# Operand sums of a seven-product scheme on GpSimd, sums of squares in PSUM, and more chunks in that scheme

## The chip, the cores and the metric

The kernel runs on one core of a Trainium2 chip. The metric is the device time of one execution in microseconds (us); a run's time is compared by the median of several executions. A core has five engines with a queue each, which run at the same time and wait for one another by semaphores: TensorE (PE in the profile, with its weight loads as PEld), VectorE (DVE), ScalarE (ACT), GpSimd (POOL) and SyncE (SP). In this kernel SP issues the stores and the DMA transposes, GpSimd issues the loads. SBUF is the working memory of 128 partitions; PSUM holds the matmuls' results in 8 banks of 128 x 2 KB.

## The reference

Four batches of 5824 rows with 256 columns go through a channel attention, and its result through a small network without nonlinearity:

```python
qn = q / (np.linalg.norm(q, axis=1, keepdims=True) + 1e-06)
kn = k / (np.linalg.norm(k, axis=1, keepdims=True) + 1e-06)
s = kn.transpose(0, 2, 1) @ qn / tau          # 256 x 256 per batch
a = softmax(s)
x = (v @ a).reshape(B * S, D)
h = (x @ w1) * (x @ w2) @ w3                  # w1, w2: 256 x 1024, w3: 1024 x 1024
out = h @ w_out                               # 1024 x 256
```

## The kernel before

The product of w3 and w_out is computed once (`w_unit`, the result is `W_sb`, 1024 x 256). For each batch the softmax matrix is multiplied into w1 and w2 (`fold`, the results are `Wf`), so that a row of the output takes two steps: a and b, each 256 to 1024 columns, their elementwise product `abh`, and `abh` times `W_sb`, called o.

**Chunks and slots.** The time is laid out by hand: the order in which the Python code emits instructions is the order in every queue. Batch b (0 to 3) has twelve chunks c: eleven of 512 rows and a small one of 192 (128 rows, and 64 rows that are paired over two batches). A chunk has eight slots, one for each 128 of the 1024 columns. In a slot `emit_ab` issues four matmuls of 512 columns into two of the four PSUM banks `ab0` to `ab3` (L587), a ScalarE copy of a to bf16 (`as`, L593) and VectorE's product with b (`abh`, L604, 128x512). Bank use comes round after two slots: a of slot s+2 overwrites a of slot s.

**The second step of a chunk** is put into a list `pend` and taken out in later slots. In a usual chunk `emit_out` adds four matmuls of 256 columns per slot (L634), 32 in all, into two PSUM tiles of the tag `out` (three banks), which ScalarE and VectorE then copy out (L655, L656), and SP stores.

**Seven products.** In the chunks that `seven(b, c)` names (four each in b=1 and b=2, ten in b=3) the second step is done by a Strassen-like scheme with seven products of half size in place of eight: `seven_products`. Each product is eight matmuls of 128 columns (L518), so 56 matmuls of 128 columns. It needs four sums of `abh` tiles (128x1024 bf16, `sum1`, and at the head of p1, p5 and p7; L534 to L551, on VectorE), combined weights (`combine_weights`, once, at the start of b=1), four ScalarE copies of a product to the output tile (`keep`, L528) and three VectorE adds (`join`, L531). Products called A, B and C take the three `out` banks. The sums share two tiles `S12` and `S34` in the pool of large tiles.

**Scores of the next batch.** While batch b runs, the 23 pairs of row blocks of batch b+1 go into the 256 x 256 score matrix: a pair is cut into units, `pair_unit`: parts 0 and 1 each have two G matmuls of 256 columns (L201) and a ScalarE square of 128x512 (L198), and in part 2 VectorE adds the squares of 128x1024 f32 to `acc` in SBUF (L210). In b=0 they are laid out by a modelled clock from 54 to 113; in b=1 and 2 by slots 4 to 71 with a weight per slot from `scores_of`, which gives few or none near a chunk of seven products. Then `norms` adds the two halves of `acc` on VectorE, GpSimd sums over the partitions (`tot`, L271, a library routine), and a chain of small steps on ScalarE and VectorE (`k_row` to `exps`) and the folds follow, at fixed distances of the modelled clock (`k_row` 5.5 after `norms`).

**GpSimd's queue** holds the loads of q, k and v. Ahead of a load stands a `gate`, a copy of one element of the latest `abh`, so that the load isn't issued before that slot, and after a load of v a `hold`, a copy of one element of the transposed v, before the next load. Transposes and stores stand in SP's queue in the order of the code.

The pool of large tiles has 22 buffers of 4 KB per partition; pieces of q, k, v and the `abh` halves come from it.

Of the kernel before, what the change touches and what calls it, by code (L numbers as in the profile page):

```python
# [12 lines left out]
F32 = DT.float32  # L13
# [6 lines left out]
BIG_BUFS = 22  # L20
# [5 lines left out]
def kernel(  # L26
# [46 lines left out]
    turns = [0]  # L73

    def bank(tag):

        if tag == "out":
            return {"tag": "out", "bufs": 3}
        turns[0] += 1
        return {"tag": f"ab{turns[0] % 4}", "bufs": 1}  # L80
# [99 lines left out]
    def score_units(n):  # L180
# [4 lines left out]
        def pair_unit(pr, part):  # L185
# [3 lines left out]
            if pr == 0 and part == 0:  # L189
                G_tiles[n] = psum.tile([P, CT, C], F32, tag="G", name=f"G_{n}", bufs=1)  # L190
                accs[n] = work.tile([P, 2, 2, C], F32, tag="acc", name=f"acc_{n}", bufs=1)
            G = G_tiles[n]
            if part < 2:
                if part == 0 and pr > 0:
                    sqs[0] = work.tile([P, 2, 2, C], F32, tag="sq", name=f"sq_{n}_{pr}", bufs=2)
                dst = accs[n] if pr == 0 else sqs[0]
                src = qt if part == 0 else kt
                nc.scalar.activation(out=dst[:, :, part, :], in_=src[:, o : o + 2, :], func=AF.Square)  # L198
# [10 lines left out]
            elif pr > 0:  # L209
                nc.vector.tensor_add(accs[n], accs[n], sqs[0])  # L210

        sqs = [None]
        for pr in range(npair):
            for part in range(3):
# [11 lines left out]
    def squares(nm, pi, slots, end=False):  # L226

        if nm not in S:
            S[nm] = psum.tile([P, CT, P], F32, tag="out", name=f"sq{nm}_0", bufs=3)
# [22 lines left out]
    def soft_units(n):  # L252
# [14 lines left out]
        def norms():  # L267
            a1 = work.tile([P, 2, C], F32, tag="acc1", name=f"acc1_{n}", bufs=1)
            nc.vector.tensor_add(a1, accs[n][:, 0], accs[n][:, 1])
# [65 lines left out]
        def sum_start():  # L335
            st["sum"] = psum.tile([P, 512], F32, tag="out" if n == 0 else "G", name=f"sum_{n}", bufs=3 if n == 0 else 1)
# [128 lines left out]
    slot = [0]  # L465
    comb = {}

    def seven(b, c):
        return c < NCH - 2 if b == B - 1 else b > 0 and c in (0, 1, 4, 7)

    def scores_of(b, s):

        j = s % FT
        after = s >= FT and seven(b, s // FT - 1)
        if (after and j < 4) or (seven(b, s // FT) and j >= FT - 2):
            return 0.0
        return 0.4 if after and j < FT - 1 else 1.0

    def combine_weights(step):
# [3 lines left out]
        if step == 0:  # L483
            comb["T"] = in_pool.tile([P, 4, 4, P], BF16, tag="big", name="comb_T", bufs=BIG_BUFS)
            for nm in ("S12", "S34"):
                comb[nm] = in_pool.tile([P, 2, 4, 2 * P], BF16, tag="big", name=f"comb_{nm}", bufs=BIG_BUFS)
# [13 lines left out]
    def seven_products(b, c, k1, k2):  # L500
# [4 lines left out]
        s1, s2 = comb["S12"][:, 0], comb["S12"][:, 1]  # L505
        s3, s4 = comb["S34"][:, 0], comb["S34"][:, 1]
# [4 lines left out]
        st = {}  # L511

        def product(nm, a, w, first=False):
            if first:
                st[nm] = psum.tile([P, 2, P], F32, tag="out", name=f"prod{nm}_{b}_{c}", bufs=3)
# [17 lines left out]
        def sum1():  # L533
# [381 lines left out]
```

## Time and profile before

| | |
|---|---|
| median of 3 runs | 563.87 us (563.73 to 564.94) |
| the profiled execution | 564.48 us |
| its span, first to last instruction | 562.7 us |
| granted TensorE clock | 1.000 |
| instructions of PE / DVE / ACT / POOL | 4180 / 693 / 683 / 163 |
| loads from memory, stores | 78.9 MB, 23.9 MB |

Up to about 46 us the first batch's q and k are loaded and their scores computed; from there to the end the slots run. b=0 ends near 181 us, b=1 near 310, b=2 near 441. In the page's list of groups a line gives line, engine, operation, output<-inputs, shapes, count, busy us and mean ns of one instruction, and after the second bar the engine's idle time ahead of it and what ended it. A matmul's mean ns is its latency: matmuls overlap, and the distance from one to the next is shorter.

### The profile page before, as it was taken

What the parts mean: (1) busy time and instruction counts of PE and PEld (TensorE: products, weight loads), DVE (VectorE), ACT (ScalarE), POOL (GpSimd) and SP (SyncE); (2) the same over time, 40 slices, a digit from 0 to 9 for tenths busy, and PEclk for the clock granted to TensorE, in tenths of its full rate; (3) what the DMA queues carried; (4) which work ended last, traced back from release to release, by engine and by line L of the source; (5) the groups of instructions that cost most, each with busy time, mean ns of one, the idle gap of its engine ahead of it and who ended that gap; (6) DMA issues with size and microseconds to landing.
All of it is one profiled execution on the core that took longest, in us unless ns stands there. A gap on an engine that the chain in (4) does not pass through costs nothing.

```text
span 562.7 us, 11089 instructions
## 1 busy us (share of the span) xinstructions
PE 552.9 (98%) x4180; PEld 356.8 (63%) x4187; DVE 424.9 (76%) x693; ACT 355.8 (63%) x683; POOL 79.8 (14%) x163
## 2 busy tenths in 40 slices
PE   8899999999999999999999999999999999999997
PEld 5764566776656566666666666666665666666665
DVE  1046745888876989899876699899877688888884
ACT  1046535777765778788665667778656566665663
POOL 4260013111021111120030100202030000100000
PEclk9999999999999999999999999999999999999999
DMA  9999899978555676675664576675760153340102
GB/s 213 212 181 209 151 179 232 224 170 187 146 127 137 122 157 137 133 162 116 150 155 109 123 161 149 138 172 86 176 133 37 76 122 76 109 94 38 76 38 93
DMA packets 75108, 77.51 MB, mean 138 GB/s; under 512 B 54192, under 2 KB 58800, under 8 KB 75056
## 3 DMA queue, kind: packets, MB, share of 16 engines
q0 software_dynamic: 15760, 38.93, 40.1%
q1 hardware_dynamic: 59008, 37.23, 21.9%
q10 hardware_dynamic: 288, 0.66, 0.4%
q8 instruction: 32, 0.52, 0.3%
q14 instruction: 20, 0.16, 0.1%
HBM read 78.91 MB, written 23.86 MB: 183 GB/s over the span
## 4 chain that ended last, share of the span: by engine, by line
PE 90%; DMA 7%; POOL 1%; DVE 1%; ACT 1%; issue 0%; POOLq 0%
PE b L587 27%; PE a L587 27%; PE o L634 17%; PE prodA L518 6%; PE G L201 5%; DMA k<-in_k_dram 5%; PE prodC L518 3%; DMA v<-in_v_dram 2%; PE fold L370 2%; PE prodB L518 1%; PE w L760 1%; POOL w L729 0%; DVE abh L604 0%; ACT as L593 0%; POOL w L728 0%
## 5 line engine op out<-in xcount | busy, mean ns | idle before, releaser
L604 DVE TENSOR_TENSOR abh<-as,b 128x512 bf16<-128x512 bf16 x352 | 240.8, 685 | 88.8 <-ACT as L593 82.5
L593 ACT CAST as<-a 128x512 bf16<-128x512 f32 (+1 forms) x384 | 216.3, 563 | 126.2 <-PE a L587 96.3
L587 PEld LDWEIGHTS <-Wf 128*128 128x128 bf16 x1536 | 144.4, 98 | 104.1 <-issue 1.7
L587 PE MATMUL a<-vT,Wf 128*128 128x512 bf16 x704 | 209.4, 379 | 0.5 <-ACT Wf L403 0.4
L587 PE MATMUL b<-vT,Wf 128*128 128x512 bf16 x704 | 209.4, 379 | 0.2 <-DVE abh L604 0.2
L634 PE MATMUL o<-W_sb,abh 128*128 128x256 bf16 x832 | 123.0, 273 | 0.0
L634 PEld LDWEIGHTS <-abh 128*128 128x128 bf16 x832 | 81.0, 98 | 41.7 <-issue 0.2
L210 DVE TENSOR_TENSOR acc<-acc,sq 128x1024 f32<-128x1024 f32 x66 | 80.4, 1219 | 0.6 <-ACT sq L198 0.6
L518 PEld LDWEIGHTS <-comb_S 128*128 128x128 bf16 x576 | 38.2, 98 | 17.0 <-DVE comb_S L534 0.2
L201 PE MATMUL G<-k,q 128*128 128x256 bf16 x276 | 48.3, 273 | 0.0
L198 ACT ACTIVATE sq<-q 128x512 f32<-128x512 bf16 x66 | 41.9, 634 | 0.0
L198 ACT ACTIVATE sq<-k 128x512 f32<-128x512 bf16 x66 | 41.5, 628 | 0.0
L528 ACT COPY osb<-prodA 128x256 f32<-128x256 f32 x72 | 26.8, 373 | 21.3 <-PE prodA L518 21.3
L518 PEld LDWEIGHTS <-abh 128*128 128x128 bf16 x432 | 28.7, 98 | 12.7
L575 POOL COPY gate_t<-abh 1x1 bf16<-1x1 bf16 x39 | 11.5, 295 | 157.1 <-DVE abh L604 156.3
L579 POOL COPY gate_t<-vT 1x1 bf16<-1x1 bf16 x16 | 4.4, 277 | 174.0 <-DMA vT<-v 174.0
L201 PEld LDWEIGHTS <-q 128*128 128x128 bf16 x276 | 26.4, 98 | 4.1
L518 PE MATMUL prodA<-comb_T,comb_S 128*128 128x128 bf16 x288 | 22.0, 219 | 0.0
L257 DVE TENSOR_TENSOR dk<-sqk,ident 128x256 f32<-128x256 f32 x1 | 0.4, 424 | 23.9 <-PE sqk L234 23.9
L656 DVE COPY osb<-o 128x512 f32<-128x512 f32 x26 | 17.8, 686 | 0.9 <-PE o L634 0.9
L598 DVE TENSOR_TENSOR left<-as,b 128x192 bf16<-128x192 bf16 x32 | 11.3, 353 | 9.5 <-ACT as L593 7.6
L655 ACT COPY osb<-o 128x512 f32<-128x512 f32 x26 | 15.2, 586 | 3.2 <-PE o L634 2.1
(116 smaller groups left out, 400.1 us busy)
## 6 DMA issues: line engine op xcount, KB each, us to landing
out_dram<-osb SPq DMA_DIRECT2D x44, 512.0 KB, 3.0
k<-in_k_dram POOLq DMA_DIRECT2D x19, 512.0 KB, 8.1
v<-in_v_dram POOLq DMA_DIRECT2D x19, 512.0 KB, 6.0
q<-in_q_dram POOLq DMA_DIRECT2D x18, 512.0 KB, 5.5
w_wout<-in_moe_w_dram POOLq DMA_DIRECT2D x1, 2048.0 KB, 23.8
k<-in_k_dram POOLq DMA_DIRECT2D x4, 320.0 KB, 7.6
v<-in_v_dram POOLq DMA_DIRECT2D x4, 320.0 KB, 4.7
q<-in_q_dram POOLq DMA_DIRECT2D x3, 320.0 KB, 4.5
```

Source lines behind the costliest of these rows:

```text
L198: nc.scalar.activation(out=dst[:, :, part, :], in_=src[:, o : o + 2, :], func=AF.Square)
L201: nc.tensor.matmul(G[:, ct, :], lhsT=qt[:, i, ct * P : (ct + 1) * P], rhs=kt[:, i, :], start=(pr == 0 and part == 0 and ct == 0), stop=(pr ...
L210: nc.vector.tensor_add(accs[n], accs[n], sqs[0])
L518: nc.tensor.matmul(st[nm][:, i, :], lhsT=a[:, j, i * P : (i + 1) * P], rhs=w[j], start=(first and j == 0 and i == 0), stop=(j == 3), skip_ ...
L528: nc.scalar.copy(quarter(r, d), st["A"])
L575: nc.gpsimd.tensor_copy(gate_t, last_ab[0][:1, :1])
L587: nc.tensor.matmul(t[:, :n], lhsT=Wf[b][:, ct, w, j * P : (j + 1) * P], rhs=rhs_of(b, c, ct), start=(ct == 0), stop=(ct == CT - 1),)
L593: nc.scalar.copy(a_sb[:, :n], tiles[0][:, :n])
L604: nc.vector.tensor_mul(ab, a_sb, tiles[1])
L634: nc.tensor.matmul(tl[h][:, o, :], lhsT=lhsT, rhs=W_sb[:, j, :], start=(j == 0 and o == 0), stop=(j == FT - 1 and (small or o == 1)), skip ...
L655: nc.scalar.copy(o[:, 0:2, :], tl[0])
L656: nc.vector.tensor_copy(o[:, 2:4, :], tl[1])
```

## The change

- The four sums of a chunk have a tile each in the pool `work` (`S1` to `S4`, one buffer). In b=0 to 2 GpSimd computes them, from a list `due_sums`, one every two slots from the chunk's end; in b=3 VectorE does, as before.
- The chunks in the scheme: 7 and 8 in b=0, 0 to 7 in b=1 and b=2, ten in b=3 as before.
- In b=0 to 2 the products begin four slots later (`LAG_FAST`), in the order p1, p6, p5, p7, p4, p3, p2, one per slot; joins run at the start of the next slot (`following`). A takes the bank `out0`, B and C `out1`.
- The sums of squares are kept in PSUM, in the third bank (`out2`), and added by VectorE in two halves of 128x512 (parts 2 and 3 of a pair). `norms` copies them with ScalarE.
- Usual chunks of b=0 to 2 (not the small one) go by `emit_half`: the first two row blocks over four slots into `out0`, then the other two into `out1`.
- Scores lie evenly over slots 42 to 78 in b=0 and 4 to 71 in b=1 and 2. The combined weights move from b=1 to b=0, the second step in b=0 starts after slot 31, some loads are moved by a few us, and the large pool has 21 buffers.

```diff
@@ -17,7 +17,8 @@
 PIECE = 8
 LAG = 2
 LAG_END = 5
-BIG_BUFS = 22
+LAG_FAST = 4
+BIG_BUFS = 21
...
-        if tag == "out":
-            return {"tag": "out", "bufs": 3}
-        turns[0] += 1
-        return {"tag": f"ab{turns[0] % 4}", "bufs": 1}
+        turns[tag] += 1
+        return {"tag": f"{tag}{turns[tag] % (4 if tag == 'ab' else 3)}", "bufs": 1}
...
-                accs[n] = work.tile([P, 2, 2, C], F32, tag="acc", name=f"acc_{n}", bufs=1)
+                accs[n] = psum.tile([P, 2, C], F32, tag="out2", name=f"acc_{n}", bufs=1)
...
             if part < 2:
-                if part == 0 and pr > 0:
+                if part == 0:
                     sqs[0] = work.tile([P, 2, 2, C], F32, tag="sq", name=f"sq_{n}_{pr}", bufs=2)
-                dst = accs[n] if pr == 0 else sqs[0]
                 src = qt if part == 0 else kt
-                nc.scalar.activation(out=dst[:, :, part, :], in_=src[:, o : o + 2, :], func=AF.Square)
+                nc.scalar.activation(out=sqs[0][:, :, part, :], in_=src[:, o : o + 2, :], func=AF.Square)
                 i = o + part
...
-            elif pr > 0:
-                nc.vector.tensor_add(accs[n], accs[n], sqs[0])
+            elif pr == 0:
+                if part == 2:
+                    nc.vector.tensor_add(accs[n], sqs[0][:, 0], sqs[0][:, 1])
+            else:
+                nc.vector.tensor_add(accs[n], accs[n], sqs[0][:, part - 2])
 
         sqs = [None]
         for pr in range(npair):
-            for part in range(3):
+            for part in range(4):
                 units.append((0.22 if part < 2 else 0.0, lambda pr=pr, part=part: pair_unit(pr, part)))
         return units
...
         def norms():
             a1 = work.tile([P, 2, C], F32, tag="acc1", name=f"acc1_{n}", bufs=1)
-            nc.vector.tensor_add(a1, accs[n][:, 0], accs[n][:, 1])
+            nc.scalar.copy(a1, accs[n])
...
     def seven(b, c):
-        return c < NCH - 2 if b == B - 1 else b > 0 and c in (0, 1, 4, 7)
-
-    def scores_of(b, s):
-
-        j = s % FT
-        after = s >= FT and seven(b, s // FT - 1)
-        if (after and j < 4) or (seven(b, s // FT) and j >= FT - 2):
-            return 0.0
-        return 0.4 if after and j < FT - 1 else 1.0
+        return c < NCH - 2 if b == B - 1 else c in (FAST if b > 0 else FAST0)
...
         if step == 0:
             comb["T"] = in_pool.tile([P, 4, 4, P], BF16, tag="big", name="comb_T", bufs=BIG_BUFS)
-            for nm in ("S12", "S34"):
-                comb[nm] = in_pool.tile([P, 2, 4, 2 * P], BF16, tag="big", name=f"comb_{nm}", bufs=BIG_BUFS)
             comb["f"] = in_pool.tile([P, 2, 4, P], F32, tag="big", name="comb_f", bufs=BIG_BUFS)
...
@@ -502,17 +497,17 @@
         T = comb["T"]
...
-        s1, s2 = comb["S12"][:, 0], comb["S12"][:, 1]
-        s3, s4 = comb["S34"][:, 0], comb["S34"][:, 1]
...
-        st = {}
+        st, sums = {}, {}
+        tags = {"A": "out0", "B": "out1", "C": "out1" if b < B - 1 else "out2"}
+        adder = nc.vector if b == B - 1 else nc.gpsimd
 
         def product(nm, a, w, first=False):
             if first:
-                st[nm] = psum.tile([P, 2, P], F32, tag="out", name=f"prod{nm}_{b}_{c}", bufs=3)
+                st[nm] = psum.tile([P, 2, P], F32, tag=tags[nm], name=f"prod{nm}_{b}_{c}", bufs=1)
             for j in range(4):
                 for i in range(2):
                     nc.tensor.matmul(
@@ -530,44 +525,62 @@
         def join(nm, r, d):
             nc.vector.tensor_add(quarter(r, d), st[nm], quarter(r, d))
 
-        def sum1():
-            nc.vector.tensor_add(s1, a21, a22)
+        def operand(i):
+
+            x = sums[i] = work.tile([P, 4, 2 * P], BF16, tag=f"S{i}", name=f"S{i}_{b}_{c}", bufs=1)
+            if i == 1:
+                adder.tensor_add(x, a21, a22)
+            else:
+                u, w = {2: (sums.get(1), a11), 3: (a11, a21), 4: (a12, sums.get(2))}[i]
+                adder.tensor_sub(x, u, w)
...
         def p5():
-            nc.vector.tensor_sub(s3, a11, a21)
-            product("C", s1, t1, True)
+            product("C", sums[1], t1, True)
 
         def p6():
-            product("A", s2, t2)
+            product("A", sums[2], t2)
             keep(0, 1)
 
         def p7():
-            nc.vector.tensor_sub(s4, a12, s2)
-            product("A", s3, t3)
+            product("A", sums[3], t3)
             keep(1, 1)
 
         def p2():
-            join("C", 1, 1)
             product("B", a12, w21, True)
 
         def p4():
-            join("B", 0, 0)
             product("A", a22, t4)
             keep(1, 0)
 
         def p3():
-            product("C", s4, w22)
-            join("C", 0, 1)
+            product("C", sums[4], w22)
+
+        def store():
             rows = out[b * N : b * N + NT * P, :].rearrange("(p i) c -> p i c", i=NT)
             nc.sync.dma_start(out=rows[:, 4 * c : 4 * c + 4, :], in_=st["o"])
 
-        return [sum1, p1, p5, p6, p7, p2, p4, p3]
+        def S(i):
+            return lambda: operand(i)
+
+        def J(*x):
+            return lambda: join(*x)
+
+        def then(fn):
+            return lambda: following.append(fn)
+
+        if b == B - 1:
+            return [S(1)], [
+                [S(2), p1], [S(3), p5], [p6], [S(4), p7], [J("C", 1, 1), p2],
+                [J("B", 0, 0), p4], [p3, J("C", 0, 1), store],
+            ]
+        return [S(1), S(2), S(3), S(4)], [
+            [p1], [p6], [p5], [p7, then(J("C", 1, 1))], [p4], [p3, then(J("C", 0, 1))], [p2, then(J("B", 0, 0)), then(store)],
+        ]
...
         if not seven(b, c):
-            pend.append((slot[0] + (FT if 0 < b < B - 1 else LAG), 1, lambda only=None: emit_out(b, c, j, ab, only)))
+            if b == B - 1 or c == NCH - 1:
+                lag = LAG if b == B - 1 else FT + LAG_FAST
+                pend.append((slot[0] + lag, 1, lambda only=None: emit_out(b, c, j, ab, only)))
+            elif j == FT - 1:
+                for i in range(FT):
+                    fn = lambda i=i, ab2=tuple(halves): emit_half(b, c, i, ab2)
+                    pend.append((slot[0] + 1 + LAG_FAST + i, 1, fn))
         elif j == FT - 1:
-            fns = seven_products(b, c, *halves)
-            fns[0]()
-            pend.extend((slot[0] + 1, 2, fn) for fn in fns[1:])
+            sums, groups = seven_products(b, c, *halves)
+            for i, fn in enumerate(sums):
+                due_sums.append((slot[0] + 2 * i, fn))
+            ready = slot[0] + 1 + (LAG_FAST if b < B - 1 else 0)
+            for i, group in enumerate(groups):
+                wait = 0 if b == B - 1 else i + (i == 6)
+                pend.append((ready + wait, 2, lambda group=group: [fn() for fn in group]))
         clock[0] += 4 * (n * MM_COL + MM_FIX)
+
+    def emit_half(b, c, i, ab2):
+
+        h, jj = divmod(i, 4)
+        if i % 4 == 0:
+            out_tiles[b, c, h] = psum.tile([P, 2, D], F32, tag=f"out{h}", name=f"o_{b}_{c}_{h}", bufs=1)
+        if i == 0:
+            out_tiles[b, c] = work.tile([P, 4, D], F32, tag="o_sb", name=f"osb_{b}_{c}", bufs=3)
+        t, o = out_tiles[b, c, h], out_tiles[b, c]
+        for j in (2 * jj, 2 * jj + 1):
+            for k in range(2):
+                nc.tensor.matmul(
+                    t[:, k, :], lhsT=ab2[j // 4][:, j % 4, (2 * h + k) * P : (2 * h + k + 1) * P], rhs=W_sb[:, j, :],
+                    start=(j == 0 and k == 0), stop=(j == FT - 1), skip_group_check=True,
+                )
+        clock[0] += 4 * (D * MM_COL + MM_FIX)
+        if i == 3:
+            nc.scalar.copy(o[:, 0:2, :], t)
+        elif i == FT - 1:
+            nc.vector.tensor_copy(o[:, 2:4, :], t)
+            rows = out[b * N : b * N + NT * P, :].rearrange("(p i) c -> p i c", i=NT)
+            nc.sync.dma_start(out=rows[:, 4 * c : 4 * c + 4, :], in_=o)
 
...
         if j == 0:
             out_tiles[b, c] = [
-                psum.tile([P, 2, D], F32, tag="out", name=f"o_{b}_{c}_{h}", bufs=3)
-                for h in range(len(lhs) if small else 2)
+                psum.tile([P, 2, D], F32, tag=tag, name=f"o_{b}_{c}_{tag}", bufs=1)
+                for tag in ((("out0", "out2") if b == B - 1 else ("out1", "out0"))[2 - len(lhs) :] if small else ("out0", "out1"))
             ]
...
-    SLOT0, SLOT1 = 4, 71
+    SLOTS0, SLOTS = (42, 78), (4, 71)
+    FAST0, FAST = (7, 8), (0, 1, 2, 3, 4, 5, 6, 7)
+    COMB, W_SLOT = 38.0, 31
...
             moves += [("v", 1, 0, 88.0), ("v", 1, 1, 98.0), ("v", 1, 2, 120.0), ("qk", 2, 0, 130.0)]
-            t0, t1 = 54.0, 113.0
         else:
-            moves = [("qk", n, 1, 1.0), ("v", b, 3, 8.0), ("qk", n, 2, 17.0), ("v", b, 4, 26.0), ("qk", n, 3, 38.0)]
-            moves += [("v", b, 5, 46.0), ("qk", n, 4, 58.0), ("qk", n, 5, 66.0)]
-            moves += [("v", n, 0, 76.0), ("v", n, 1, 86.0), ("v", n, 2, 96.0), ("qk", n + 1, 0, 108.0)]
+            moves = [("qk", n, 1, 1.0), ("v", b, 3, 8.0), ("qk", n, 2, 21.0), ("v", b, 4, 26.0), ("qk", n, 3, 38.0)]
+            moves += [("v", b, 5, 46.0), ("qk", n, 4, 56.0), ("qk", n, 5, 66.0)]
+            moves += [("v", n, 0, 74.0), ("v", n, 1, 86.0), ("v", n, 2, 99.0), ("qk", n + 1, 0, 112.0)]
             moves = [m for m in moves if m[1] < B]
...
-        if b == 1:
+        if b == 0:
             for i in range(4):
-                at(3.0 + 2.6 * i, 0.0, lambda i=i: combine_weights(i))
+                at(COMB + 2.6 * i, 0.0, lambda i=i: combine_weights(i))
...
         units = score_units(n)
         soft = soft_units(n)
...
+        first, last = SLOTS if b > 0 else SLOTS0
+        for s in range(first, last):
+            lo_, hi_ = (-(-len(units) * (x - first) // (last - first)) for x in (s, s + 1))
+            by_slot.append((s, units[lo_:hi_]))
...
     for b in range(B):
@@ -860,18 +891,21 @@
         for c in range(NCH):
             for j in range(FT):
                 run_due()
-                if b > 0:
-                    scores_due(c * FT + j)
+                while following:
+                    following.pop(0)()
+                scores_due(c * FT + j)
                 emit_ab(b, c, j)
                 lag = 0
                 if b == B - 1 and c >= NCH - 2:
                     lag = LAG_END if c == NCH - 1 else LAG + (LAG_END - LAG) * (j + 1) // FT
                 room = 2
-                while w_ready[0] and len(pend) > lag and pend[0][0] <= slot[0] and pend[0][1] <= room:
+                while slot[0] > W_SLOT and len(pend) > lag and pend[0][0] <= slot[0] and pend[0][1] <= room:
                     _, size, fn = pend.pop(0)
                     fn()
                     room -= size
                     run_due()
+                while due_sums and due_sums[0][0] <= slot[0]:
+                    due_sums.pop(0)[1]()
         run_due(1e9)
```

## The prediction, made before the changed kernel ran

> **What bounds the kernel now.** I read the page's shares, slices and chain first, then the windows of the two middle batches, then the groups by form, then GpSimd's timeline.
>
> ```profile
> PE 552.9 (98%) x4180; PEld 356.8 (63%) x4187; DVE 424.9 (76%) x693; ACT 355.8 (63%) x683; POOL 79.8 (14%) x163
> PE   8899999999999999999999999999999999999997
> PEclk9999999999999999999999999999999999999999
> ```
>
> TensorE is full at the full clock, GpSimd almost idle. The windows' columns are length, then busy time of PE, PEld, DVE, ACT and POOL; these two are batches b=1 and b=2:
>
> ```profile
> 176.00:310.00 134.00, 133.72 (x985) 85.62 (x984) 113.49 (x182) 95.69 (x187) 20.00 (x40) 1.00 0.64 138
> 310.00:441.00 131.00, 130.90 (x960) 83.58 (x959) 108.35 (x172) 92.60 (x178) 17.58 (x36) 1.00 0.60 130
> ```
>
> A busy PE could still hide gaps, so I look at the steps of the chain that ended last (start, length, what), first in a usual chunk, then in a chunk of seven products:
>
> ```profile
> 78.23 0.87 PE o L634 x8
> 79.10 0.43 PE a L587 x2
> 79.53 0.43 PE b L587 x2
> 79.96 0.87 PE o L634 x8
> ...
> 200.71 0.45 PE prodA L518 x8
> ...
> 202.02 0.45 PE prodC L518 x8
> ```
>
> and at the idle time before each group (last column):
>
> ```profile
> L604 DVE TENSOR_TENSOR abh<-as,b 128x512 bf16<-128x512 bf16 x352 | 240.8, 685 | 88.8 <-ACT as L593 82.5
> L587 PE MATMUL a<-vT,Wf 128*128 128x512 bf16 x704 | 209.4, 379 | 0.5 <-ACT Wf L403 0.4
> L634 PE MATMUL o<-W_sb,abh 128*128 128x256 bf16 x832 | 123.0, 273 | 0.0
> L210 DVE TENSOR_TENSOR acc<-acc,sq 128x1024 f32<-128x1024 f32 x66 | 80.4, 1219 | 0.6 <-ACT sq L198 0.6
> L531 DVE TENSOR_TENSOR osb<-prodC,osb 128x256 f32<-128x256 f32 x36 | 15.0, 418 | 0.0
> L538 DVE TENSOR_TENSOR comb_S<-comb_S,abh 128x1024 bf16<-128x1024 bf16 x18 | 12.3, 685 | 0.0
> ```
>
> The matmuls wait for nothing. The time is the sum of the matmuls' steps: whatever shortens them is gained in full, whatever makes TensorE wait is lost in full. GpSimd's queue:
>
> ```profile
> 37.67 0.41 POOL L774 PARTITION_ALL_REDUCE lib<-ones_f  x1
> ...
> 329.96 0.18 POOL L579 COPY gate_t<-vT 1x1 bf16<-1x1 bf16 x1 [8.46 <-DMA vT<-v]
> 330.29 0.18 POOL L575 COPY gate_t<-abh 1x1 bf16<-1x1 bf16 x1
> 330.83 0.53 POOL L120 DMA_DIRECT2D q<-in_q_dram  x1 [0.36 <-PE a L587]
> 331.35 0.54 POOL L120 DMA_DIRECT2D k<-in_k_dram  x1
> ...
> 414.37 3.23 POOL L271 PARTITION_ALL_REDUCE tot<-acc  x1 [2.83 <-DVE acc L269]
> ```
>
> A load costs it 0.53, a hold 0.33, a gate 0.5 to the next start. No elementwise operation of any size runs there yet.
>
> **Part 1, ten more chunks of seven products.** Seven-product chunks were 4+4+10 (b=1,2,3), and become 2+8+8+10. One step of a and b plus eight o matmuls takes 79.96-78.23 = 1.73; with a product instead, 202.02-200.71 = 1.31. a and b alone are 4 x 0.2165 = 0.866 (379 ns is latency; the chain shows 0.43 for two). So eight o's are 0.87 and a product 0.445. A usual chunk: 4 x 0.87 = 3.48. Seven products: 7 x 0.445 = 3.12. Gain 0.36, between 3.3 and 3.7 for ten with the rounding: **3.5 us**. The matmuls keep their place in the one PE order, so it is gained whole if no new wait comes.
>
> **Part 2, the squares' sums in PSUM.** The add of 128x1024 (L210, 1.219) becomes two of 128x512 with one operand and the output in PSUM. No VectorE row writes PSUM. Bounds: 0.685 (L604, same size, one operand in PSUM) and 1.219 (L210, twice the elements). I take 0.69, as the shape is L604's. Per chunk of eight slots in b=1,2 there are 23 pairs x 8/67 = 2.75 pairs. VectorE: 8 x 0.685 + 3 joins x 0.418 + 5.5 x 0.69 = 10.5. TensorE: 8 x 0.866 + 3.12 + 2.75 x 4 x 0.109 = 11.25. VectorE stays under, so cost **0**, hidden by the matmuls; the cover is gone when an add costs over (11.25-5.48-1.25)/5.5 = 0.82. At 1.219 it would be 13.4 against 11.25: 2.2 x 16 chunks = 35 us. The four sums that leave VectorE (4 x 0.685 per chunk, L538) are what makes room. ScalarE: 8 x 0.585 + 4 keeps x 0.373 + 5.5 squares x 0.63 = 9.6, hidden too. The sum of squares' last add moves to ScalarE as a copy of 128x512 (0.59, L655's row), off the path.
>
> **Part 3, the sums on GpSimd.** Eighteen chunks x 4 sums of 128x1024, price X unknown. From below 0.685 (the same sums on VectorE). From above 3.23 (the all-reduce of 128x512 f32, which crosses partitions as well). They are far apart and neither is near: by work the sum is L538's, by engine the all-reduce's; I take the middle, **2.0**. What is allowed: in b=1 the first sum can start when chunk 0's last product is written, 0.9 after slot 8 starts; the last deadline is the p3 of chunk 7, in slot 73.6. That is 65.6 slots x 11.25/8 = 92.3 - 0.9 = 91.4. In the queue between stand 15 loads x 0.53 = 8.0 and 12 gates and holds x 0.4 = 4.9, and 32 sums. 32X + 12.9 = 91.4 gives X = **2.45**; above it TensorE waits 32(X-2.45) per batch, in two batches. At 2.0 the queue has 14 us to spare: cost 0. Single deadlines are easier: from the chunk's end to p6 are 5.6 slots or 7.9 us for two sums, to p3 9.6 slots or 13.5 for four. The other side of it: a GpSimd that runs late issues its loads late, and the hold behind v's last piece (8.2 to 10 us from load to transposed in before, with nothing queued behind it) now stands in front of a second sum: it idles GpSimd up to 3.4 (9.4 less three sums), within the 14.
> A page of the Trainium skill speaks against this part: GPSIMD Engine Reference, section 3.1, has an add of 2048 f32 at 4497 ns, twice VectorE's, and keeps elementwise work off this engine. By it X is an estimated 2.25; 32 x 2.25 + 12.9 = 84.9 of 91.4, still no wait, but with half the margin. No row of before shows it.
>
> **Part 4, switching GpSimd's code.** In the built order an extra configuring instruction now stands before the first sum and before each all-reduce: six more than the one at 37.5. There, the last load issue ended at 37.54 and the all-reduce began at 37.67: R = 0.13, if the code was not simply there already. From above: 6.0, the median of a 512 KB load on the page. I take 0.13, the one row of it. It bites at the start of b=1,2: after the load in slot 6 (gate and load 1.0, product 0.9 late) R and two sums must fit till p6 of chunk 0: 6.6 x 1.41 - 1.9 = 7.4. With X = 2.0, R up to 3.4 is free; 6.0 costs 2.6 per batch. Before the all-reduce R has 15.3 - 4X = 7.3 free (from chunk 7's end in slot 64 to the row k_row in slot 77, plus 1.4 for the spare banks, less 0.9 and 3.2), so it costs nothing there.
> The same reference, section 2.1, gives about 6 us (5.95 measured) for the first call after a load of code. By the row the sum is 561.0; by that rule it is 561.0 + 2 x 2.55 = 566.1, slower than before.
>
> **Part 5, banks and order.** Products and o now alternate in two banks. The keep of p1 must end before p6 starts, one a-b step later (0.866); keep 0.373 behind an as of 0.585. Before, p6 and p7 stood just so and L518 waited 0.0. I cost it 0, bound 0.1 x 2 x 28 chunks = 5.6. The late folds of b=0, the combined weights now in b=0 (four adds of 0.685 beside 1.7 us steps) and the later stores on SP have slack in their stages: 0 to 1, I take **0.5** for all.
>
> **Sum.** The profiled execution took 564.48 (span 562.7, 1.8 around it). 564.5 - 3.5 + 0.5 = 561.5. It lies 0.6 over the median of the runs (563.87), so the forecast is **561.0** (560.9 rounded), own range 560.0 to 562.5.
>
> **Rivals.**
> A, GpSimd becomes the bound (the slower side). One mechanism: sums late at TensorE's p6, p7, p3 in b=1,2. It decides from X = 2.45 + 3.0/64 = 2.50, where the gain is eaten. Halfway between 2.45 and 3.23, X = 2.84: 64 x 0.39 = 25, time 586. For it: the only real computation on this engine takes 3.2 for half the columns. Against: that one crosses partitions. Chance 0.20.
> B, code switches cost microseconds: R of 6.0 gives 2 x 2.6 = 5.2, time 566; R of 5 gives 3.2, time 564. For it: the kernel calls its library once early for nothing else. Against: 0.13 in the row. Chance 0.16: 0.10 slower, 0.06 no change.
> C, short waits at the two banks or at VectorE's adds into PSUM, 0.05 to 0.15 per product pair: 2 to 5 us, time 563 to 565. Against: the 0.0 of L518. Chance 0.08, no change.
> D, it does not do what it says: the narrow products are held by their weight loads (98 ns each against steps of 56). Against: eight already go in 0.45. Time 563.9. Chance 0.04.
>
> **How the numbers follow.** Forecast 0.52. A measurement here tells 0.2% (1.1 us) from no change. Faster 0.52; same 0.06 + 0.08 + 0.04 = 0.18; slower 0.20 + 0.10 = 0.30. The range runs from 560.0 to 569: it holds the forecast, B, C, D and the mild end of A (X up to 2.57), and leaves out some 0.17 of A and a little below.
>
> **What would show it.** Right: L518 at 0.445 per eight with idle near 0; the sums' row on POOL near 2; PE idle before prodA and prodC none; the adds into PSUM near 0.69; the reduce done before its kr. Wrong: weight loads of the products waiting for POOL, most in b=1,2 (A), a gap on POOL before the first sum of a batch (B), waits for ScalarE's keep (C), products slower than 0.445 (D).

## The result, and the profile after

| | before | after |
|---|---|---|
| median of the runs, us | 564.2 (563.7 to 565.5, six) | 592.9 (592.2 to 600.5, six) |
| profiled execution, us | 564.5 | 592.2 |
| its span, us | 562.7 | 590.5 |
| mean granted TensorE clock in it | 1.00 | 0.986 |

The changed kernel is slower: ratio 1.0535, interval 1.048 to 1.059. The forecast was 561.0, its range 560.0 to 569.0. The page of the kernel after: its shares, and three rows of its slices.

```profile
PE 555.7 (94%) x4427; PEld 357.6 (61%) x4427; DVE 416.8 (71%) x747; ACT 361.7 (61%) x716; POOL 227.4 (39%) x235
...
PE   8899999998999599989999959999988999999997
...
POOL 4250014025622388698630169799830000000000
PEclk9999999999999899999999979999998999999999
```

TensorE was at 9 in nearly every slice before. Now two slices are at 5 (the 14th and 24th), each at the start of a batch; POOL is at 2 and 3, and at 0 and 1, just there or ahead of them. The clock dips in the same two, and in the 31st. The groups, with the idle time before each at the end:

```profile
L600 PE MATMUL a<-vT,Wf 128*128 128x512 bf16 x704 | 211.5, 382 | 5.1 <-ACT as L606 4.6
...
L211 DVE TENSOR_TENSOR acc<-acc,sq 128x512 f32<-128x512 f32 x132 | 91.6, 694 | 8.1 <-ACT sq L196 7.2
L513 PEld LDWEIGHTS <-S 128*128 128x128 bf16 x896 | 60.7, 100 | 46.0 <-POOL S L535 19.9
...
L648 PE MATMUL o<-W_sb,abh 128*128 128x256 bf16 x480 | 69.5, 274 | 0.0
...
L513 PE MATMUL prodA<-comb_T,S 128*128 128x128 bf16 x448 | 35.2, 223 | 17.4 <-POOL S L535 17.3
L532 POOL TENSOR_TENSOR S<-abh,abh 128x1024 bf16<-128x1024 bf16 x18 | 38.2, 2123 | 31.0 <-DVE abh L617 21.8
...
L535 POOL TENSOR_TENSOR S<-S,abh 128x1024 bf16<-128x1024 bf16 x18 | 38.3, 2130 | 1.0
```

The two prices that the forecast hung on came out near what it took: a sum 2.13 us (2.0 taken), an add into PSUM 0.694 (0.69 taken). Yet the products wait for the sums, and the view of waits (total, times, longest) says in how few places:

```profile
PE prodA L513 <- POOL S L535: 17.3, 4, 7.1
ACT kr L293 <- POOL tot L272: 10.2, 3, 6.5
```

Four waits make 17.3 us. A queue that is too full would be late at every chunk; this is late once or twice a batch. GpSimd's timeline (start, length, in brackets the idle time in front) shows why:

```profile
191.77 0.53 POOL L119 DMA_DIRECT2D v<-in_v_dram  x1 [0.28 <-issue]
201.24 2.10 POOL L532 TENSOR_TENSOR S<-abh,abh 128x1024 bf16<-128x1024 bf16 x1 [8.94 <-DVE acc L211]
...
245.13 2.12 POOL L532 TENSOR_TENSOR S<-abh,abh 128x1024 bf16<-128x1024 bf16 x1 [0.74 <-DVE abh L617]
250.44 0.18 POOL L592 COPY gate_t<-vTt 1x1 bf16<-1x1 bf16 x1 [3.18 <-DMA vTt<-v]
...
252.28 2.13 POOL L535 TENSOR_TENSOR S<-S,abh 128x1024 bf16<-128x1024 bf16 x1
...
432.66 0.57 POOL L119 DMA_DIRECT2D v<-in_v_dram  x1 [0.36 <-issue]
440.64 3.25 POOL L272 PARTITION_ALL_REDUCE tot<-acc  x1 [7.41 <-issue]
```

Between a load and the first sum of a batch GpSimd does nothing for 8.9 us, and before the all-reduce for 7.4. Only the configuring instruction stands there; the releaser in the bracket (an add on VectorE, or the issue) is merely the last event seen. The inputs don't hold it up: the all-reduce's, a copy by ScalarE, is done at 432.4. The view of a line of code has the configuring instruction, two records for each change (shortest, median and longest in ns, first and last start), here for the first sum's line and the all-reduce's:

```profile
L532 POOLq MODIFY_POOL_CONFIG  x6: 37/40/42, 129.6 to 333.7; - x6
L272 POOLq MODIFY_POOL_CONFIG  x6: 11/11/37, 158.5 to 433.5; - x6
```

They are over in some 0.04 us, and the engine then stands still; on what the time goes, no record shows. In batches zero, one and two this idle time is 8.8, 8.9 and 8.7 us before the first sum, and 5.9, 6.1 and 7.4 before the all-reduce. At 250.44 a hold, which waits for v's transposes, stands between S1 and S2 of one chunk. What the first gap does to TensorE, in the chain of waits (start, length, what):

```profile
201.24 2.10 POOL S L532
...
203.43 2.13 POOL S L535
...
205.60 1.04 PE prodA L513 x8
206.63 0.85 PE a L600 x2
207.49 0.85 PE b L600 x2
208.34 0.85 PE prodC L513 x8
...
209.47 0.43 PE a L600 x2
```

p6 waits for both sums, and behind the stall every step takes 0.85 where 0.43 is usual, for 3.6 us: TensorE is at half its pace. In two windows around such stalls (columns as before, the clock third from the end):

```profile
180.00:312.00 132.00, 122.19 (x966) 76.08 (x965) 97.46 (x173) 90.18 (x179) 85.24 (x72) 0.97 0.63 133
...
440.00:470.00 30.00, 25.22 (x168) 15.96 (x167) 16.41 (x36) 15.66 (x35) 3.25 (x1) 0.94 0.17 62
```

Counted from start to start of successive matmuls, less the usual step of that shape, from 46 us on, TensorE loses 33.7 us (2.2 before): 7.25 and 6.1 at p6 of the first chunk of batches one and two, 4.8 at the end of batch two where ScalarE's kr (the first step of `k_row`) waits for the late all-reduce and the copies of a stand behind it, 2.45 and 2.2 at holds between S1 and S2 (at 142 and 252), about 6.2 of half pace behind the three long stalls, the rest small. 33.7 - 2.2 less the 3.5 that the products were to gain is 28.0; the two profiled executions differ by 27.7, the medians by 28.7.

### The profile page after: what moved, and what is told of

Same layout as the page of the kernel before. It is cut to its first block, busy times and chain, and to the rows that moved or that the text cites. A ratio compares the mean times of both kernels' runs of the same rounds, so it can differ in the third digit from the quotient of the medians.

```text
span 590.5 us, 11766 instructions
## 1 busy us (share of the span) xinstructions
PE 555.7 (94%) x4427; PEld 357.6 (61%) x4427; DVE 416.8 (71%) x747; ACT 361.7 (61%) x716; POOL 227.4 (39%) x235
## 4 chain that ended last, share of the span: by engine, by line
PE 74%; DMA 12%; POOL 5%; DVE 3%; issue 3%; ACT 2%; SPq 0%; POOLq 0%; DVEq 0%; ACTq 0%
PE b L600 23%; PE a L600 23%; PE prodA L513 9%; DMA k<-in_k_dram 6%; PE o L648 5%; PE prodC L513 4%; PE G L199 4%; DMA v<-in_v_dram 4%; PE prodB L513 2%; DMA vT<-v 2%; POOL tot L272 2%; DVE abh L617 2%; ACT as L606 2%; PE o_out L679 2%; POOL S L535 1%
## 5 line engine op out<-in xcount | busy, mean ns | idle before, releaser
L211 DVE TENSOR_TENSOR acc<-acc,sq 128x512 f32<-128x512 f32 x132 | 91.6, 694 | 8.1 <-ACT sq L196 7.2
L513 PEld LDWEIGHTS <-S 128*128 128x128 bf16 x896 | 60.7, 100 | 46.0 <-POOL S L535 19.9
L523 ACT COPY osb<-prodA 128x256 f32<-128x256 f32 x112 | 41.7, 372 | 49.0 <-PE prodA L513 48.9
L648 PE MATMUL o<-W_sb,abh 128*128 128x256 bf16 x480 | 69.5, 274 | 0.0
L648 PEld LDWEIGHTS <-abh 128*128 128x128 bf16 x480 | 46.8, 98 | 21.8 <-issue 0.6
L513 PEld LDWEIGHTS <-abh 128*128 128x128 bf16 x672 | 44.6, 98 | 20.1 <-issue 0.4
L513 PE MATMUL prodA<-comb_T,S 128*128 128x128 bf16 x448 | 35.2, 223 | 17.4 <-POOL S L535 17.3
L532 POOL TENSOR_TENSOR S<-abh,abh 128x1024 bf16<-128x1024 bf16 x18 | 38.2, 2123 | 31.0 <-DVE abh L617 21.8
L535 POOL TENSOR_TENSOR S<-S,abh 128x1024 bf16<-128x1024 bf16 x18 | 38.3, 2130 | 1.0
L535 POOL TENSOR_TENSOR S<-abh 128x1024 bf16<-128x1024 bf16 x18 | 38.3, 2130 | 0.0
L535 POOL TENSOR_TENSOR S<-abh,S 128x1024 bf16<-128x1024 bf16 x18 | 38.3, 2127 | 0.1
```

What stands on the lines that cost most here:

```text
L211: nc.vector.tensor_add(accs[n], accs[n], sqs[0][:, part - 2])
L513: nc.tensor.matmul(st[nm][:, i, :], lhsT=a[:, j, i * P : (i + 1) * P], rhs=w[j], start=(first and j == 0 and i == 0), stop=(j == 3), skip_ ...
L523: nc.scalar.copy(quarter(r, d), st["A"])
L532: adder.tensor_add(x, a21, a22)
L535: adder.tensor_sub(x, u, w)
L648: nc.tensor.matmul(t[:, k, :], lhsT=ab2[j // 4][:, j % 4, (2 * h + k) * P : (2 * h + k + 1) * P], rhs=W_sb[:, j, :], start=(j == 0 and k = ...
```

## The experiments

Medians against runs of before on the same chip. None of the kernels leaves work out; e7 does a sum twice.

**e1, the switch moved up.** On after:

```diff
             nc.gpsimd.partition_all_reduce(...)
+            if n < B - 1:
+                nc.gpsimd.tensor_add(tiny_o, ones_f[:1, :], ones_f[:1, :])
```

> The changed kernel with one more instruction on GpSimd: a one-element add right behind the all-reduce of b=0 and b=1, so that the switch of code from the all-reduce to the sums happens there and not ahead of the first sum of b=1 and b=2. Theory (code switches): in the changed kernel the first sums of b=1 and b=2 start 8.9 and 8.7 us after the load ahead of them, TensorE stands 7.2 and 6.1 us before p6 and then runs some 4 us more than usual at a low clock; all that goes, 592.9 - 17.5 = 575 (572 to 579). The all-reduce of b=2 still comes 7 us late. Rival (GpSimd's queue is too full for the sums, X above its limit): one more small instruction helps nothing, 593 or more.

591.1 us, ratio 1.048 (1.046 to 1.050): the theory's number missed by 16. GpSimd's timeline in e1:

```profile
168.72 3.25 POOL L273 PARTITION_ALL_REDUCE tot<-acc  x1 [6.01 <-DVE abh L620]
178.97 0.18 POOL L278 TENSOR_TENSOR tiny_o<-ones_f 1x1 f32<-1x1 f32 x1 [7.00 <-issue]
...
189.85 0.54 POOL L120 DMA_DIRECT2D q<-in_q_dram  x1
...
206.56 2.12 POOL L535 TENSOR_TENSOR S<-abh,abh 128x1024 bf16<-128x1024 bf16 x1 [0.17 <-DVE abh L620]
```

The gap did leave the first sum (0.17 before it), and batch two's stall there fell from 6.1 to 0.3. But the switch now stood in front of a load of v, the hold on v's transposes and the next q and k, which went out at 189.85 (178.58 in after), so the squares and the score matmuls (G) of batch one waited:

```profile
PE G L200 <- DMA k<-in_k_dram: 8.2, 1, 8.2
```

Besides, a new wait of 3.4 us came at 124, in a batch in which nothing was moved; see e11.

**e2, no switch after the first.** On after: the partition sum by TensorE (a 128 x 128 matrix of ones) in place of GpSimd's all-reduce, so that only sums need code there.

```diff
+        def norm_mm():
+            m = psum.tile([P, 2, C], F32, tag="out2", name=f"tot_{n}", bufs=1)
+            nc.tensor.matmul(m..., lhsT=ones_pp, rhs=st["a1"]..., start=True, stop=True)
-            [(0.0, 0.0, norms), (0.0, 5.5, k_row)]
+            [(0.0, 0.0, norms), (0.9, 2.5, norm_mm), (0.0, 5.5, k_row)]
```

> The changed kernel with the sum over partitions done by TensorE (a matmul of 128x512 f32 with ones into the bank of the sums of squares) in place of GpSimd's all-reduce, and no early library call: no code is switched while the slots run. Theory (code switches): the three long stalls (7.2, 6.1, 4.8) and the low clock behind them (about 6.2) go, 24.3 us; three f32 matmuls cost up to 0.9 each; 592.9 - 24.3 + 2.7 = 571 (568 to 574), with the two stalls of 2.2 and 2.4 behind the holds left. Rival (GpSimd's queue too full): the all-reduce's 3.2 per batch is all that leaves the queue, 585 to 593, with waits for sums all through b=1 and b=2.

571.9 us, ratio 1.013 (1.011 to 1.015): as the theory had it, 21 us less than after. The two middle batches in e2, clock 1.00 again:

```profile
180.00:312.00 132.00, 129.45 (x1030) 81.46 (x1030) 102.85 (x183) 95.64 (x189) 81.62 (x71) 1.00 0.68 141
312.00:440.00 128.00, 127.68 (x1037) 81.91 (x1036) 100.37 (x182) 93.23 (x189) 80.36 (x67) 1.00 0.64 133
```

With 64 sums of 2.13 us still on GpSimd, TensorE is nearly full. So the sums' length is not the loss; the switches are.

**e3, the sums on VectorE.** On after: `adder = nc.vector` for every batch.

> The changed kernel with all sums on VectorE: GpSimd has no elementwise work and no code is switched. Theory: the switches' 24 us go, but VectorE has 10.5 + 4 x 0.685 = 13.3 us of work in a chunk of 11.25 us of matmuls, 2.0 us over in 16 chunks, 32 us: 560.7 + 32 = 593 (583 to 598). Rival (VectorE has room, and the loss is GpSimd's alone): 561 to 566.

577.9 us, ratio 1.024 (1.022 to 1.027): no switches, and 15 us less than after, but neither the theory's 583 to 598 nor the rival's 561 to 566. VectorE is too full, as the theory had it, but costs less: it is busy 117.6 of batch one's 132 us, and the loss comes in short waits for it all through (20.2 us by the count above, none over 2.7).

**e4, switches put into before.** On before, a one-element add in front of each all-reduce:

```diff
+            nc.gpsimd.tensor_add(tiny_o, ones_f[:1, :], ones_f[:1, :])
             nc.gpsimd.partition_all_reduce(...)
```

> The kernel before with a one-element add on GpSimd ahead of each of the three all-reduces, so that the code is switched there and back; nothing else is changed, and no result uses the add. Theory (code switches of 8.8 and 5.6 to 7.1 us): in b=1 and b=2 the all-reduce ends some 15 us later than it is read, less 1.4 that the spare banks cover, plus 2 to 2.5 of low clock each; in b=0 about 1: 564.2 + 2 x 16 + 1 = 597 (588 to 602). Rival (switches cost 0.13 us as at 37.5 in the kernel before): 564.2, no change.

597.4 us (a single run): a hit. Three one-element adds cost 33 us, because the code changes twice at each; the second of the three:

```profile
297.16 0.18 POOL L272 TENSOR_TENSOR tiny_o<-ones_f 1x1 f32<-1x1 f32 x1 [8.66 <-issue]
303.21 3.25 POOL L273 PARTITION_ALL_REDUCE tot<-acc  x1 [5.87 <-issue]
```

This alone, with none of the change's other parts, makes before as slow as after.

**e5, the holds moved.** On e2, two load times: `("v", 1, 1, 98.0)` to 105.0 and `("qk", n, 4, 56.0)` to 62.0.

> The kernel e2_no_switch (571.9 us) with two load times moved and nothing else: in batch zero the load of v's second piece from 98 to 105, and in batches one and two that of q and k's fifth piece from 56 to 62. So no hold (the one-element copy that waits for v's transposes) stands between S1 and S2 of a chunk any more. Theory: each of the two holds cost TensorE what p6 waited for S2 in e2, 2.38 us at 142.8 and 2.43 at 246.4, and the first stall also some 1.6 us at a low TensorE clock just behind it: 571.9 - 6.4 = 565.5 us (563 to 568). Rival: the transposes are late for somebody else as well, or the later loads are, and the stall only moves on: 570 to 573.

576.3 us, ratio 1.021 (1.019 to 1.023): missed, slower than e2 and outside the rival's range too. In batch zero it did what it should (the wait of 2.4 us at 143 and the half pace behind it are gone). In batches one and two q and k went out later, and the score matmuls waited for them; batch one in e5:

```profile
PE G L199 <- DMA k<-in_k_dram: 3.4, 1, 3.4
```

**e6, the partition sum in bf16.** On e5: `a1` and the ones in bf16.

> e5_no_switch_holds_moved with the partition sum by TensorE in bf16 (the ones and the copied squares' sums are bf16) in place of f32. In e2 each of the three f32 sums took two passes, 0.49 and 0.43 us from start to next start, together 0.91; one pass of a 512 column bf16 matmul takes 0.22. Theory (TensorE is the bound, so what it no longer does comes off the time): 3 x 0.69 = 2.1 us under e5, about 563.4 us (561 to 566), that is level with before or a little faster. Rival: the sum lies in time that TensorE waits anyway: same as e5 within 0.5.

572.9 us, ratio 1.016 (1.014 to 1.017). 3.3 us under e5 where 2.1 were expected; the direction is right, the number 563.4 fell with e5's. By the count above e6 loses 1.3 us less than e5 (13.1 for 14.4), mostly the half pace behind the stall at 249, which e5 shows and e6 does not; with the 2.1 that makes the 3.3.

**e7, five sums a chunk.** On e5, in batches one and two:

```diff
                 adder.tensor_sub(x, u, w)
+                if i == 3 and 0 < b < B - 1:
+                    adder.tensor_sub(x, u, w)
```

> e5_no_switch_holds_moved with S3 of every chunk of batches one and two computed twice, so five sums of 2.13 us on GpSimd for each chunk in place of four. It tests the queue limit of the prediction (32 X + 12.9 = 91.4 per batch, limit 2.45 us a sum against 2.13 measured: 10 us of slack per batch). Theory: 8 x 2.13 = 17.0 us more per batch against 10 of slack, so GpSimd becomes the bound for 7 us in each of two batches: e5 + 14 us (8 to 20), about 579. Rival: the queue has much more room than the sum says: e5 + 0 to 3; or no room at all: e5 + 34.

588.0 us, ratio 1.042 (1.039 to 1.046; two runs, 586.1 and 590.0): 11.7 over e5, inside the theory's 8 to 20 and far from both rivals. That fits a slack of some 11 us a batch (17.0 less half of 11.7), where the prediction had 10. By the count above 6.7 us of it are waits for sums, in seven places, and 3.0 longer waits for k, whose loads stand in the same queue.

**e8, the holds placed.** On e6: `("qk", n, 4, 58.5 if n == 2 else 56.0)`, so the hold of batch one lies between S2 and S3.

> e6_bf16_norms (572.9 us) with q and k's fifth piece back at 56 in batch two and at 58.5 in batch one, so that the hold there lies between S2 and S3, and the load as early as it can. In e5 and e6 these two loads went out some 3 us later than in e2 and the squares of batch one and two (matmuls into G) waited for them: 3.70 us at 248.5 and 3.44 at 382.8, with some 1.4 us at a low TensorE clock behind the second. Theory (both waits go, and S2 is no longer late): 572.9 - 8.6 = 564.3 us (562.5 to 567), level with before. Rival: one of the two waits stays in another place: 568 to 572.

566.0 us, ratio 1.0033 (1.0021 to 1.0045): 6.9 under e6 and inside the theory's range. One wait was left, as e8's waits in batch one show:

```profile
PE G L201 <- DMA k<-in_k_dram: 1.6, 1, 1.6
```

**e9, eight fewer such chunks.** On e8: `FAST = (0, 1, 4, 7)` for batches one and two, so their other chunks go the long way.

> e8_holds_placed with chunks 0, 1, 4 and 7 alone by seven products in batches one and two, as before the change had it, so eight such chunks fewer. It measures what a chunk by seven products is worth: the prediction had 3.5 us for ten chunks (sixteen matmuls of 128 columns at 0.056 against eight of 256 at 0.109 each step, seven steps for eight, 0.35 a chunk). Theory: e8 + 8 x 0.35 = e8 + 2.8 us (2 to 3.8). Rival: the products' chunks lose their gain in waits for the sums or banks, so nothing or a gain: e8 - 2 to e8 + 1.

567.6 us, ratio 1.0067 (1.0042 to 1.0091): only 1.6 over e8. In the profiled executions the spans differ by 5.6 us, of which 3.0 is more waiting by the count above (the wait for k is 2.8 there), and 2.6 the longer work: 0.33 a chunk, against 0.35 in the prediction. By the medians it is 0.2, between the theory's range and the rival's, so the size rests on that one execution, the slowest of e9's six.

**e10, the switch in idle time.** On after: the one-element add right behind the load of the next batch's first q and k.

> The kernel after (592.9 us) with a one-element add on GpSimd right behind the load of the next batch's first q and k piece in batches zero and one, where GpSimd then has some 10 us without work. The code for the sums comes in there, and not in front of batch one's and two's first sum, and no load or hold stands behind it that is due, as there did in e1_switch_early. Theory: the stalls of 7.25 us at 198 and 6.1 at 340 go, and some 5 us of low TensorE clock behind them; those before the all-reduce and the holds stay: 592.9 - 18 = 575 us (571 to 579). Rival (the switches' price is not the cause, or it only moves): 588 to 593.

583.2 us, ratio 1.035 (1.033 to 1.037): between the two. GpSimd's timeline in e10:

```profile
319.72 0.18 POOL L865 TENSOR_TENSOR tiny_o<-ones_f 1x1 f32<-1x1 f32 x1 [10.68 <-issue]
...
331.54 2.12 POOL L533 TENSOR_TENSOR S<-abh,abh 128x1024 bf16<-128x1024 bf16 x1 [0.27 <-DVE abh L618]
```

The stalls of 7.25 and 6.1 are gone. What keeps it from 575 is again a wait of 3.6 us at 124 and the half pace behind it.

**e11, without the new tile.** On after, the same add as e10's, but written into `gate_t`, so nothing new is allotted.

> e10_switch_in_idle (583.2 us) with the one-element add written into the gate's own element, so without a new one-element tile among the constants. e1, e4 and e10, which all have this new tile, show v's transposes in batch zero later than after does (4.3 to 4.4 us from issue to landing against 3.9 in the median, the hold's release at 94 to 95 against 91), and e1 and e10 a TensorE wait of 3.4 and 3.6 us at 124 for v in place of 0.6. Theory: the tile, that is the place in SBUF of what is allotted after it, is the cause: the wait at 124 is back at 0.6, with its low clock and the 0.7 more at 147 some 5 us: 578 us (576.5 to 580), which with the 5 us added is also what e10 was to give. Rival: the tile has nothing to do with it (the chip, or the run): 582 to 584.5.

577.6 us, ratio 1.026 (1.024 to 1.029): the theory's number. The hold's release is back at 92.3 (94.8 in e10, 91.0 in after), the median transpose of v in the first 125 us back at 3.9 us (4.4), the wait at 124 at 0.9. So the two code switches before the sums cost after 15 us. That the tile is to blame rests on e10 against e11, on two chips where before takes 564.4 and 563.8; e14, without the tile, has a median of 4.3 us too and no wait at 124, so the transposes' time does not settle it.

**e12, v's last piece earlier.** On e8, in batch one: `("v", b, 5, 42.5 ...)` in place of 46.0, and `("qk", n, 4, 56.0)`.

> e8_holds_placed (566.0 us) with v's last piece of batch one loaded at 42.5 in place of 46, so that its transposes have landed before the hold, and q and k's fifth piece of batch one back at 56. In e8 the squares of batch one still waited 1.75 us for k at 248. Theory: this wait goes, and nothing else is late: 564.3 us (563 to 565.5), level with before. Rival: the earlier load of v's piece runs into that of q and k's fourth piece, and another wait comes: 566 to 568.

564.8 us, ratio 1.0013 (1.0004 to 1.0022): a hit, the wait at 248 is gone, and level with before within what a measurement tells.

**e13, batch zero plain.** On e12: `FAST0 = ()`, and one add into `gate_t` at 62.0 to bring the code in.

> e12_v_earlier (564.8 us) with no chunk of batch zero by seven products (two in e12), and the code for the sums brought in by a one-element add behind the load of v's last piece in batch zero, where GpSimd then waits some 20 us for v's transposes. It leaves out the change's part for the first batch. Theory: the two chunks are worth 2 x 0.33 = 0.7 us by e9, but the waits in batch zero that before did not have (0.97 at 124, 0.62 at 157, 1.24 at 170 in e12, together 2.8) come with the fuller queues there, and most go: e12 + 0.7 - 1.9 = 563.6 us (562.5 to 564.6). Rival: the waits of batch zero have another cause, only the 0.7 is lost: 565.5 (565 to 566.5).

563.8 us, ratio 0.9995 (0.9986 to 1.0004): a hit in the number, level with before. The mechanism holds in part: of the waits it names, that at 124 stayed (1.19 us), of the others 0.53 is left, at 172. In that place of the softmax chain, batch zero's two chunks seem to cost more than they bring; the intervals of e12 and e13 just touch. In e13 the program has a single change of code, its first, and GpSimd's timeline shows what that costs:

```profile
101.66 0.56 POOL L121 DMA_DIRECT2D v<-in_v_dram  x1
102.32 0.18 POOL L862 TENSOR_TENSOR gate_t<-ones_f 1x1 bf16<-1x1 f32 x1
```

The configuring instruction stands between these two, and there is next to no gap.

**e14, the softmax chain earlier.** On e12: `SLOTS0 = (42, 75)` in place of (42, 78). In e12 ScalarE's exponential stood in front of a copy of a out of its bank (an eviction) and waited for VectorE, beside matmuls too short to cover it:

```profile
168.97 0.51 ACT L337 ACTIVATE e<-s,r 128x256 bf16<-128x256 f32 x1 [1.09 <-DVE s L332]
...
170.72 0.32 PE L605 MATMUL b<-vTt,Wf 128*128 128x192 bf16 x2 [0.36 <-DVE abh L622]
```

> e12_v_earlier with the squares of batch zero ended three slots earlier (75 in place of 78), so that the softmax chain behind them runs beside matmuls of 512 columns and not beside those of 192. In e12 at 169 and 171 ScalarE's exponential stands in front of an eviction and waits 1.09 and 0.60 us for VectorE's s, and TensorE waits 1.24 us in all for the evictions there. Theory: these 1.2 us go, e12 - 1.2 = 563.6 us (562.8 to 564.5). Rival: the denser squares make v's or the evictions' wait at 124 or 157 longer: 564.5 to 566.

563.1 us, ratio 0.9983 (0.9974 to 0.9992): the theory's direction, and 1.7 us under e12 where 1.2 was expected. The waits at 170 and 171 are gone, but so are those at 124 and 157, and 0.8 at 152 and 0.4 at 175 are new; the count falls by 1.2 in all. This is the one version faster than before, by 1.0 us; the interval allows 0.5 to 1.5, so it is at the edge of what the prediction said a measurement here can tell (1.1).

## Why the prediction was wrong, by its steps

The step that failed is part 4, "I take 0.13, the one row of it". That row is the early library call, the program's first change, where no code was waited for; a first change costs nothing in e13 either. The prediction's own doubt, "if the code was not simply there already", was the right one. Its upper bound, the 6.0 of a load, was no bound either. Measured are 8.7 to 8.9 us in front of a sum and 5.9 to 7.4 in front of an all-reduce, at each of the six later changes. The rest of that step's working holds: "R up to 3.4 is free" becomes 3.1 with sums of 2.13, so 8.8 gives 5.7 us per batch; 7.25 and 6.1 were lost. So rival B named the mechanism and sized it by too low a bound.

GPSIMD Engine Reference of the Trainium skill, section 2.1, gives 5.95 us for the first call after a load of code. The all-reduce's 5.9 to 7.4 come near it, the sums' 8.8 are half as much again, and the measurements decide. By the page the forecast would have been an estimated 566.1: slower than before, by some 2 of the 29 us.

"Before the all-reduce R has 15.3 - 4X = 7.3 free", "so it costs nothing there", held in batches zero and one and failed in batch two. (Two sums of the prediction are off by little and change nothing: the terms given for the 15.3 make 15.6, and in part 3 twelve gates and holds of 0.4 make 4.8 and not 4.9.) It counted four sums between the last chunk and the row, and not what else is queued there: in batch two a hold of 1.9, a gate and a load of v. TensorE waited 4.8 us there. The two places part by experiment: hiding the changes before the sums of batches one and two gives 15 us (e11); doing away with every change but the first gives 21 (e2, which pays some 2.7 for its f32 matmuls).

Part 3's price was right (2.13 for 2.0), with luck, as it was the middle of two bounds far apart; its queue sum fits e7. Wrong was the hold, "up to 3.4 (9.4 less three sums), within the 14": its wait came out at 3.2 (at 250), but slack over a whole batch does not help one chunk. The hold's wait falls between S1 and S2, whose p6 is due 7.9 us after the chunk's end; two chunks paid 2.45 and 2.2. (At 142 the first sum is late as well; e2, where it is not, lost 2.4 there by the hold alone.) By the same page's section 3.1 a sum was an estimated 2.25; measured 2.13.

Part 1: right in mechanism; 0.33 a chunk for 0.35, by e9's profiled execution. Before and after agree: their spans less what TensorE loses by the count are 560.5 and 556.8, 3.7 for ten chunks. Part 2: right, 0.694 for 0.69, and no long wait for VectorE (0.9 us in all). Part 5: TensorE waits for no `keep`, so nothing is late at the banks; its 0.5 for the late chain of batch zero is too little once the stalls are gone (1.2 in e12, removed in e14).

Not in the prediction at all: TensorE at half pace behind a long stall, some 6 us, a fifth of the loss. Behind a long stall "whatever makes TensorE wait is lost in full" falls short: it is lost in full, and more. The Trainium skill states it: TensorE: Matmul & The Clock Gate, Part 1, has the clock at half after an idle window of some 3.4 us and full again after a busy one as long. The rows agree in part. In after the three stalls over 3.4 us are followed by half pace (0.85 for 0.43), for 3.6, 5.8 and 3.3 us, and those of 2.45 and 2.2 are not. Over all runs the length of the stall does not decide it: half pace stands behind stalls of 2.1 us (e1, at 257) and 2.4 (e2, at 143), and none behind 3.7 (e6, at 249) and 3.4 (e10, at 249). What decides it there is open. I had not weighed it because I foresaw no long stall.

Why the gain of 3.5 is not whole in e14 either: its partition sums cost TensorE about 0.7, and 2.2 us more waits than in before are left, 0.8 of them at 152 in batch zero, where a matmul of b waits for VectorE's product. 3.5 - 2.9 leaves 0.6; 1.0 was measured.

## What to carry to other kernels

An engine that is idle is not free for a new kind of operation: count how often its code would change, and look for one extra instruction in the built order with a gap behind it; a price read at the first change says nothing of the later ones. Give a new wait in a queue to the nearest deadline behind it, not to the slack of the batch. In a kernel whose bound engine is full, a load moved by 3 us is already a stall (e5).

## What was not expected of the hardware

- GpSimd's code change was paid at every alternation between all-reduce and elementwise add but the program's first, for one element as for 131072. The gap depends on what stands ahead: before an add 8.7 to 10.8 us behind a load and 7.0 to 7.5 behind an all-reduce, before an all-reduce 5.9 to 7.0 behind an add and 7.2 to 7.5 behind a load (after, e1, e4, e10, e11). The one-element copies of the gates, and the loads it issues, run with no such gap in between.
- Behind stalls of 4.8 to 7.25 us in after, TensorE's steps took twice as long (0.85 for 0.43) for 3.3 to 5.8 us. Stalls of 2.1 to 3.7 us had it in some runs and places and not in others.
- e10 and e11 differ in one new one-element tile among the constants, and by 5.6 us. The median transpose of v in the first 125 us took 4.3 to 4.4 us in the three kernels with it (four transposes each), and 3.9 in all others but e14, the fastest, which has 4.3. Whether the tile does it, by moving the addresses of later tiles, was not tried by itself and stays open.
- An f32 matmul of 512 columns stands in the trace as two, 0.49 and 0.43 us to the next start (e2): together some four times the 0.216 of one in bf16.
